# Chunk-selected attention with an ELU MLP on one core: V through the hardware DMA queue with a cast on GpSimd, and weight loads split and queued behind the casts

## The chip, the cores and the metric

The kernel runs on one core of one Trainium2 chip. The time is the device time of one execution in microseconds (us). A "span" is the time from the first to the last instruction of the one profiled execution. All profiled executions shown here are fast runs.

## The reference, cut to what matters

Attention over 4 batches of 8 heads, sequence 768, head dimension 64. For each query, an upper bound of the score is computed for each chunk of 32 keys (from the chunk's minimum and maximum), and only the six best chunks take part. The result, 3072 tokens of 512, goes through an MLP.

```python
k_min = np.min(k_chunks, axis=3); k_max = np.max(k_chunks, axis=3)
ub = np.sum(np.maximum(q[:, :, :, None, :] * k_min[:, :, None, :, :], q[:, :, :, None, :] * k_max[:, :, None, :, :]), axis=-1)
top_chunks = np.argsort(np.where(causal, ub, -1e9), axis=-1)[..., -6:]
...                                   # masked softmax over the selected chunks
attn @ v                              # (4, 8, 768, 64) -> x (3072, 512)
h = x @ w_in                          # (512, 2048)
g = np.where(h > 0, h, np.exp(np.minimum(h, 0)) - 1)
return g @ w_out                      # (2048, 512)
```

Inputs are fp32; V is 6.3 MB and the two weight matrices are 8.4 MB together.

## The kernel before

Heads are handled in 16 pairs. `load` brings K and Q of a pair, `prep` transposes them on TensorE, `select` makes the selection mask of two pairs, and `attend` computes scores, softmax and output. A scheduler orders each engine's queue at build time, so the order of the code is not the order of the queues.

K and Q come over SyncE's hardware queue (called the SP queue below); V and the weights are cast from fp32 to bf16 while they are transferred, which is done from GpSimd's software queue:

```python
def load(t):
    ...
    for h in range(2):
        nc.sync.dma_start(out=k_pair[:, :, h, :], in_=k[b, 2 * r + h].rearrange("(n p) d -> p n d", p=P))
    for h in range(2):
        nc.sync.dma_start(out=q_pair[:, :, h, :], in_=q[b, 2 * r + h].rearrange("(n p) d -> p n d", p=P))

def load_v(t):
    for h in range(2):
        nc.gpsimd.dma_start(out=vexts[t % NSET][:, :, h, 0:D], in_=v[b, 2 * r + h].rearrange("(n p) d -> p n d", p=P))
```

The mask reaches the score matmul's operands through four small DMAs (27 KB each) that stand on the same SP queue as K and Q:

```python
def select(g):
    ...
    nc.vector.transpose(out=selT, in_=sb[:, :, :].rearrange("p b c -> p (b c)"))
    for j in range(2):
        s = (2 * g + j) % NSET
        nc.sync.dma_start(out=rhsA[s][64:64 + NCH, Q0:S], in_=selT[64 * j:64 * j + NCH, :])
        nc.sync.dma_start(out=rhsB[s][0:NCH, Q0:S], in_=selT[64 * j + 32:64 * j + 32 + NCH, :])
```

The weights are loaded almost at once:

```python
def prep_group(g):
    for j in range(2):
        t = 2 * g + j
        if t + 2 < npairs:
            lds[t + 2] = load(t + 2)
        load_v(t)
        prep(t)

prep_group(0)
load_w_in()
select(0)
prep_group(1)
load_w_out()
for g in range(ng):
    attend(2 * g)
    ...
```

The softmax here doesn't subtract the row's maximum and nothing guards it: scores larger than these inputs give would overflow.

## Time and profile before

| reading | value |
|---|---|
| time, median of 3 | 397.43 us (396.59 to 397.96) |
| span of the profiled run | 394.6 us |
| TensorE (PE) busy | 317.5 us, 80% |
| PE busy before 60 us | 23.7 us |
| PE busy after 60 us | 294 of 335 us, 88% |

The first fence is from the profile page: the span in 40 slices of 9.9 us; a digit is the busy share in tenths, PEclk the granted TensorE clock in tenths, DMA the mean busy share of the 16 DMA engines in tenths, and the last row the GB/s that they moved.

```profile
PE   1562068678869869999998788999999988979886
PEclk9995559959998989999999699999999999999999
DMA  9999993543643733930233034101100010200102
GB/s 174 209 186 189 192 207 21 85 108 24 87 104 21 113 81 26 173 94 2 80 28 26 2 26 54 53 2 45 38 13 2 27 53 2 80 2 35 44 2 80
```

In the first six slices the DMA engines are busy all the time and PE is nearly idle in slices four and five. The next fence is the timeline of that stretch: start, length, engine ("SPq" is the SP queue issuing a DMA), line, operation; at the end the idle time before it and what ended it. Lines 82 and 85 load K and Q, lines 217 and 218 the mask.

```profile
16.18 9.96 SPq L85 DMA_DIRECT2D q_pair<-in_q_dram  x2
26.26 5.23 SPq L82 DMA_DIRECT2D k_pair<-in_k_dram  x2
28.02 0.77 DVE L214 STREAM_TRANSPOSE selT<-selb_171 128x576 bf16<-128x576 bf16 x1
31.59 9.38 SPq L85 DMA_DIRECT2D q_pair<-in_q_dram  x2
41.07 5.13 SPq L82 DMA_DIRECT2D k_pair<-in_k_dram  x2
46.30 0.86 SPq L217 DMA_DIRECT2D rhsA_119<-selT  x1
49.00 0.58 PE L243 MATMUL sps<-rhsA_119,lhsA_117 128*128 128x384 bf16 x2 [15.38 <-DMA rhsA_119<-selT]
```

The mask selT is ready at 28.8 us. Its DMA is issued at 46.3 us, because the loads of q3, k4, q4 and k5 (pair 3's Q, pair 4's K and so on) stand before it in the in-order queue, and each of these lines, two issues of 192 KB, takes 5 to 10 us where an unhindered one takes about 1.1 us. PE waits 15.4 us for the mask.

### The profile page before, as it was taken

The numbers are of one execution on the slowest core, as the hardware profiler recorded it, in microseconds if no ns is written. First come the engines' busy times: TensorE is split into PE (matmuls) and PEld (weight loads), VectorE is DVE, ScalarE is ACT, GpSimd is POOL, SyncE is SP. The second block draws the span as 40 slices with busy tenths as digits, with TensorE's granted clock in tenths as the row PEclk, the third lists the DMA queues.
The fourth block names the chain that finished last, engine by engine and source line by source line (L and its number), as shares of the span: only waits on it lengthen the run. The fifth ranks groups of instructions, "written<-read, shape, count | busy, mean of one in ns | idle before, by whom it ended". The sixth has DMA issues, their size and how long they took to land.

```text
span 394.6 us, 6477 instructions
## 1 busy us (share of the span) xinstructions
PE 317.5 (80%) x2272; PEld 175.1 (44%) x2272; DVE 205.0 (52%) x594; ACT 226.5 (57%) x489; POOL 116.2 (29%) x244
## 2 busy tenths in 40 slices
PE   1562068678869869999998788999999988979886
PEld 1331034444544545554555454554556444444442
DVE  7462026637638737555286396372686345252550
ACT  2633086696896894785378956672589143251430
POOL 7651001201413322243033233251133134151430
PEclk9995559959998989999999699999999999999999
DMA  9999993543643733930233034101100010200102
GB/s 174 209 186 189 192 207 21 85 108 24 87 104 21 113 81 26 173 94 2 80 28 26 2 26 54 53 2 45 38 13 2 27 53 2 80 2 35 44 2 80
DMA packets 82592, 27.52 MB, mean 70 GB/s; under 512 B 76160, under 2 KB 78976, under 8 KB 82560
## 3 DMA queue, kind: packets, MB, share of 16 engines
q1 hardware_dynamic: 54784, 19.77, 20.4%
q0 software_dynamic: 27776, 7.34, 18.2%
q8 instruction: 18, 0.29, 0.3%
q14 instruction: 14, 0.11, 0.1%
HBM read 27.26 MB, written 6.29 MB: 85 GB/s over the span
## 4 chain that ended last, share of the span: by engine, by line
issue 30%; PE 24%; ACT 18%; POOL 16%; DVE 8%; SPq 3%; DMA 1%; POOLq 0%; ACTq 0%
POOL m_sb L301 13%; PE o_ps L308 9%; ACT pt L246 5%; PE sps L243 4%; PE ub L200 3%; DVE gT L303 2%; PE h_ps L295 2%; SPq L85 2%; PE psK L162 2%; PE psQ L182 2%; ACT QTf L187 1%; SPq L82 1%; ACT e_sb L299 1%; ACT rhsB_120 L189 1%; ACT lhsB_118 L169 1%
## 5 line engine op out<-in xcount | busy, mean ns | idle before, releaser
L295 PE MATMUL h_ps<-xt,w_in_sb 128*128 128x384 bf16 x512 | 105.3, 327 | 12.1 <-DVE gT L303 11.5
L301 POOL TENSOR_SCALAR m_sb<-e_sb 128x384 f32<-128x384 f32 x128 | 65.6, 516 | 155.2 <-ACT e_sb L299 143.8
L246 ACT ACTIVATE pt<-sps 128x384 bf16<-128x384 f32 (+1 forms) x160 | 80.4, 534 | 53.4 <-PE sps L243 51.5
L303 DVE SCALAR_TENSOR_TENSOR gT<-h_ps,m_sb 128x384 bf16<-128x384 f32 x128 | 70.4, 554 | 41.4 <-POOL m_sb L301 38.1
L308 PE MATMUL o_ps<-w_out_sb,gT 128*128 128x512 bf16 x384 | 88.1, 379 | 0.0
L299 ACT ACTIVATE e_sb<-h_ps 128x384 f32<-128x384 f32 x128 | 62.3, 496 | 40.4 <-PE h_ps L295 38.6
L295 PEld LDWEIGHTS <-w_in_sb 128*128 128x128 bf16 x512 | 48.3, 97 | 47.3 <-issue 20.2
L308 PEld LDWEIGHTS <-gT 128*128 128x128 bf16 x384 | 37.2, 98 | 40.8 <-issue 1.0
L314 DVE COPY o_sb<-o_ps 128x512 f32<-128x512 f32 x16 | 11.1, 691 | 53.1 <-PE o_ps L308 53.0
L273 PEld LDWEIGHTS <-pt 128*128 128x128 bf16 x672 | 29.3, 103 | 17.5 <-DVE pt L255 8.0
L182 PE MATMUL psQ<-ident_f,q_pair 128*128 128x128 f32 x96 | 21.0, 338 | 17.3 <-ACT lhsB_118 L169 7.3
L162 PE MATMUL psK<-ident_f,k_pair 128*128 128x128 f32 x96 | 19.2, 317 | 11.2 <-DMA k_pair<-in_k_dram 4.6
L312 ACT ACTIVATE o_sb<-o_ps 128x512 f32<-128x512 f32 x8 | 4.8, 597 | 39.0 <-PE o_ps L308 39.0
L190 DVE TENSOR_SCALAR Qrl<-QTf 128x576 f32<-128x576 f32 x16 | 7.5, 469 | 35.1 <-ACT QTf L187 35.1
L182 PEld LDWEIGHTS psQ<-ident_f,q_pair 128*128 128x128 f32 x96 | 12.3, 164 | 28.5 <-ACT lhsB_118 L169 10.1
L243 PE MATMUL sps<-rhsA_119,lhsA_117 128*128 128x384 bf16 (+2 forms) x36 | 9.9, 315 | 18.4 <-DMA rhsA_119<-selT 15.4
L255 DVE TENSOR_TENSOR pt<-pt,tri_168 128x512 bf16<-128x512 bf16 x32 | 13.5, 421 | 13.4 <-ACT pt L246 13.4
L162 PEld LDWEIGHTS psK<-ident_f,k_pair 128*128 128x128 f32 x96 | 11.5, 157 | 19.6 <-ACT rhsB_120 L189 5.6
L249 ACT ACTIVATE pt<-sps 128x512 bf16<-128x512 f32 x32 | 19.3, 604 | 1.4 <-PE sps L243 1.3
L285 DVE COPY xt<-pxt 128x384 bf16<-128x384 bf16 x32 | 11.3, 352 | 16.2 <-PE pxt L284 15.8
L165 DVE TENSOR_REDUCE kmm<-psK 128x12 f32<-128x384 f32 x32 | 17.6, 549 | 3.9 <-PE psK L162 3.4
L166 DVE TENSOR_REDUCE kmm<-psK 128x12 f32<-128x384 f32 x32 | 17.4, 545 | 0.0
(220 smaller groups left out, 418.2 us busy)
## 6 DMA issues: line engine op xcount, KB each, us to landing
k_pair<-in_k_dram SPq DMA_DIRECT2D x32, 192.0 KB
q_pair<-in_q_dram SPq DMA_DIRECT2D x32, 192.0 KB
out_dram<-o_sb SPq DMA_DIRECT2D x24, 256.0 KB
w_in_sb<-in_moe_w_in_dram POOLq DMA_DIRECT2D x4, 512.0 KB, 8.9
w_out_sb<-in_moe_w_out_dram POOLq DMA_DIRECT2D x4, 512.0 KB, 17.3
vext_116<-in_v_dram POOLq DMA_DIRECT2D x8, 96.0 KB, 3.4
vext_122<-in_v_dram POOLq DMA_DIRECT2D x8, 96.0 KB, 3.6
vext_128<-in_v_dram POOLq DMA_DIRECT2D x8, 96.0 KB, 3.4
```

Source lines behind the costliest of these rows:

```text
L162: nc.tensor.transpose(ps[:, P * n:P * (n + 1)], k_pair[:, 3 * h + n], ident_f)
L165: nc.vector.tensor_reduce(out=kmm[:, 0, cs], in_=pv, axis=AX.X, op=AOT.min)
L182: nc.tensor.transpose(ps[:, P * n:P * (n + 1)], q_pair[:, 3 * h + n], ident_f)
L243: nc.tensor.matmul(sps[:, o + pc:o + pc + w], lhsT=lhs[hd][:, P * kb:P * (kb + 1)], rhs=rhs[hd][:, c0:c0 + w], start=True, stop=True)
L246: nc.scalar.activation(out=pt[:, hd, 0:wtot], in_=sps[:, 0:wtot], func=AF.Exp, scale=SCALE)
L249: nc.scalar.activation(out=pt[:, :, 0:256], in_=sps[:, :].rearrange("p (h w) -> p h w", h=2), func=AF.Exp, scale=SCALE)
L273: nc.tensor.matmul(o3[:, hd, qi, :], lhsT=pt[:, hd, P * qt + off:P * qt + off + P], rhs=vexts[s][:, kb, hd, :], start=(kb == 0), stop=(kb ...
L295: nc.tensor.matmul(hw, lhsT=w_in_sb[:, kk, P * fc:P * (fc + 1)], rhs=xT[NPAIR * b + kk][:, ts], start=(kk == 0), stop=(kk == NKK - 1))
L299: nc.scalar.activation(out=e_sb, in_=hw, func=AF.Exp)
L301: nc.gpsimd.tensor_scalar(out=m_sb, in0=e_sb, scalar1=-1.0, scalar2=1.0, op0=AOT.add, op1=AOT.mult)
L303: nc.vector.scalar_tensor_tensor(out=gT[:, fc, :], in0=hw, scalar=0.0, in1=m_sb, op0=AOT.max, op1=AOT.min)
L308: nc.tensor.matmul(o_ps, lhsT=gT[:, fc, P * tt:P * (tt + 1)], rhs=w_out_sb[:, fc, :], start=(fc == 0), stop=(fc == NFC - 1))
```

## The change

The intent is to take V off GpSimd's software DMA and to keep the weights out of the way of the first loads. V is loaded as fp32 over the SP queue and cast on GpSimd; the weights are cut in quarters, queued on GpSimd behind the V casts of pairs 2 to 5; two pools shrink to make room for the fp32 V.

```diff
-    ptpool = pool("ptpool", 14)
+    ptpool = pool("ptpool", 10)
-    xtpool = pool("xtpool", 12)
+    xtpool = pool("xtpool", 10)
+    def load_v(t):
+        b, r = divmod(t, NPAIR)
+        v_pair = ldpool.tile([P, NQT, 2, D], F32, name="v_pair")
+        for h in range(2):
+            nc.sync.dma_start(out=v_pair[:, :, h, :],
+                              in_=v[b, 2 * r + h].rearrange("(n p) d -> p n d", p=P))
+        return v_pair
+    ldv = {t: load_v(t) for t in range(2)}
-    def load_v(t):
-        ...                                   # the casting DMA on GpSimd
+    def cast_v(t):
+        return nc.gpsimd.tensor_scalar(out=vexts[t % NSET][:, :, :, 0:D], in0=ldv.pop(t), scalar1=1.0,
+                                       scalar2=0.0, op0=AOT.mult, op1=AOT.add)
...
+    wload = {2: [lambda: load_w_in(0), lambda: load_w_in(1)],
+             3: [lambda: load_w_in(2), lambda: load_w_in(3)],
+             4: [lambda: load_w_out(0), lambda: load_w_out(1)],
+             5: [lambda: load_w_out(2), lambda: load_w_out(3)]}
     def prep_group(g):
         ...
                 lds[t + 2] = load(t + 2)
-            load_v(t)
+                ldv[t + 2] = load_v(t + 2)
             prep(t)
+            cast = cast_v(t)
+            if t in wload:
+                with tc.issue_after(cast.ins):
+                    for f in wload[t]:
+                        f()
-    load_w_in()
-    load_w_out()
```

More of the change, by code (lines that the diff above doesn't have):

```diff
@@ L106 @@
         kst.append(const.tile([P, 2, 64], F32, name=f"kst{s}"))
-    def load_v(t):
-        b, r = divmod(t, NPAIR)
-        for h in range(2):
-            nc.gpsimd.dma_start(out=vexts[t % NSET][:, :, h, 0:D],
-                                in_=v[b, 2 * r + h].rearrange("(n p) d -> p n d", p=P))
+    def cast_v(t):
+        return nc.gpsimd.tensor_scalar(out=vexts[t % NSET][:, :, :, 0:D], in0=ldv.pop(t), scalar1=1.0,
+                                       scalar2=0.0, op0=AOT.mult, op1=AOT.add)
     for s in range(NSET):
@@ L141, with load_w_in, load_w_out @@
     w_out_sb = const.tile([P, NFC, DMODEL], BF16, name="w_out_sb")
-    def load_w_in():
-        for kk in range(NKK):
-            nc.gpsimd.dma_start(out=w_in_sb[:, kk, :], in_=moe_w_in[P * kk:P * (kk + 1), :])
-    def load_w_out():
-        wo = moe_w_out.rearrange("(k p) f -> p k f", p=P)
-        for i in range(4):
-            nc.gpsimd.dma_start(out=w_out_sb[:, 4 * i:4 * i + 4, :], in_=wo[:, 4 * i:4 * i + 4, :])
+    wi = moe_w_in.rearrange("(k p) f -> p k f", p=P)
+    wo = moe_w_out.rearrange("(k p) f -> p k f", p=P)
+    def load_w_in(i):
+        nc.gpsimd.dma_start(out=w_in_sb[:, :, 512 * i:512 * (i + 1)], in_=wi[:, :, 512 * i:512 * (i + 1)])
+    def load_w_out(i):
+        nc.gpsimd.dma_start(out=w_out_sb[:, 4 * i:4 * i + 4, :], in_=wo[:, 4 * i:4 * i + 4, :])
     qf = {}
```

## The prediction

> **What bounds the kernel now.** Median 397.4 us, profiled span 394.6. The stage table shows two regimes. After 60 us PE is busy 294 of 335 us (88%) and DMA shares fall to 0.1-0.7: PE-bound. Before 60 us PE is busy only 23.7 us while the DMA share is 0.9-1.3 at 176-209 GB/s: DMA-bound.
>
> The timeline shows how this costs time. The first selection mask selT is ready at 28.8 us, but its four small DMAs stand on the in-order SP queue behind q3, k4, q4 and k5. Those issues are back-pressured (q3 10.0 us, k4 5.2, q4 9.4, k5 5.1, against 1.1 us unhindered), because the weights (8.4 MB in HBM) share the DMA engines. The mask is issued at 46.3 us, and the first score matmul starts at 49.0 us after PE idled 15.4 us (releaser: DMA rhsA<-selT).
>
> The Trainium skill, "DMA: Bandwidth & Descriptors", section "Queues, rings and completion order", says each DMA engine round-robins between queue rows; the trace agrees: from 7 to 46 us the SP queue moved only some 3.1 MB (80 GB/s).
>
> **What the change does.**
> - V goes to the SP queue as fp32: 6.3 MB. From the queue table (23.5 ns per hardware packet) and an unchanged 24,600 packets I estimate 2.2 us of all 16 engines per pair, about what V cost before.
> - GpSimd loses two V issues per pair (1.69 us) and gains one 128x768 cast; from the 0.51 us of the 128x384 m_sb I estimate 1.0-1.6 us. Neutral.
> - Weights start only after the cast of pair 2's V, about 20 us instead of 11; w_out's halves wait for attention of pairs 0 and 1.
> - In the built order the first mask DMAs now follow pair 3's V and precede k4. Ahead of them are 4.7 MB. At 190 GB/s with one w_in quarter competing, I estimate they issue at 28-30 us, just as selT is ready, and land by 32-33 us.
> - ptpool 14 to 10, xtpool 12 to 10: somewhat less run-ahead; the built PE order still interleaves much alike.
>
> **On the critical path.** Attention starts at about 33 instead of 49 us: 16 us, and everything behind it shifts. Given back: the second mask sits behind pairs 4, 5, k6 and w_in, which I estimate free at 47-55 us where it is wanted at about 51: 0-4 us; smaller pools and casts in the GpSimd order, 0-3 us. The first w_in columns land near 30 us, before their first matmul; w_out long before use.
>
> **Predicted: 382 us, 80% range 374 to 390. Faster by over 2%: 0.87; within 2%: 0.10; slower: 0.03.**
>
> **What would show each step.** (1) Timeline: first score matmul at 31-35 us, SP issues up to v3 short (1-3 us), selT's DMA issued within 2 us of selT. (2) PE idle before the first score matmul falls from 15 to under 4 us. (3) The cast lasts 1.0-1.6 us and GpSimd is no oftener the releaser. (4) Stage table: DMA share near 1 until 55-60 us; PE busy from attention's start to the end about 294 us over 330-336 us.
>
> **What would make it wrong.** The cast takes far longer (strided bf16 output, DVE beside it) and, in order, delays m_sb or the kst of the next selection; late V delays kst of pair 1, so selT; weights and pairs 4-6 collide and stall group 1's mask or w_in by over 5 us; smaller pools break overlap late, where PE is the limit.

## The result, and the profile after

| | before | after |
|---|---|---|
| time, median of 3 | 397.43 us | 379.73 us (377.84 to 379.96) |
| span of the profiled run | 394.6 us | 378.3 us |
| mask issued / first score matmul | 46.30 / 49.00 us | 28.43 / 34.92 us |
| first score matmul to the end | 345.6 us | 343.4 us |

The ratio is 0.9543 (95% interval 0.9489 to 0.9597). Ratios here are the mean time of one kernel's fast runs over that of the other's fast runs of the same rounds, so they are not quite the ratio of the quoted medians. Executions over 1.5% slower than the fastest of the same kernel are left out of the means. When the changed kernel was run again on another chip it gave 380.46 us and 0.9594 (0.9561 to 0.9627).

The same rows of the page for the changed kernel (slices of 9.5 us):

```profile
PE   1476876889599999599997799999999989979886
PEclk9995697589989999989998999999999999999999
DMA  9949999935914526501000000102000100101002
GB/s 205 277 74 192 203 181 177 280 71 118 209 42 98 125 71 161 117 2 55 30 12 2 1 14 28 58 0 83 5 11 2 57 29 26 58 3 55 28 2 83
```

PE no longer stands still in slices four and five. The DMA engines are busy to about 76 us instead of 60, and rest in slice three. The timeline of the changed kernel (line 93 loads V, 118 is the cast, 154 loads w_in, 189 transposes Q, 224 is the mask, 250 the scores):

```profile
16.23 1.30 SPq L93 DMA_DIRECT2D v_pair<-in_v_dram  x2
18.19 0.84 POOL L118 TENSOR_SCALAR vext_134<-v_pair 128x768 bf16<-128x768 f32 x1
18.97 0.98 POOL L154 DMA_DIRECT2D w_in_sb<-in_moe_w_in_dram  x1
27.64 0.77 DVE L221 STREAM_TRANSPOSE selT<-selb_177 128x576 bf16<-128x576 bf16 x1
28.43 0.86 SPq L224 DMA_DIRECT2D rhsA_125<-selT  x1
34.23 0.90 PE L189 MATMUL psQ<-ident_f,q_pair 128*128 128x128 f32 x3 [0.88 <-ACT lhsB_142 L176]
34.92 0.63 PE L250 MATMUL sps<-rhsA_125,lhsA_123 128*128 128x384 bf16 x2
```

The first weight quarter is issued at 19.0 us, when all loads of pairs 0 to 3 have already been issued (the last one, pair 3's V, took 1.3 us). The mask follows its transpose at once, and PE comes to the first score matmul straight from a transpose, with no wait for the mask.

Of the 16.3 us by which the span shortened, 14.1 us had been gained by the first score matmul (49.00 to 34.92) and 2.2 us after it (345.6 to 343.4). The queue table, before and then after (packets, bytes, time of the packets as a share of 16 engines' span; q1 is hardware, q0 software):

```profile
q1 hardware_dynamic: 54784, 19.77, 20.4%
q0 software_dynamic: 27776, 7.34, 18.2%
```

```profile
q1 hardware_dynamic: 79872, 26.06, 27.7%
q0 software_dynamic: 4224, 4.19, 7.1%
```

Share times span gives 80.5 us (q1) and 71.8 us (q0) before, 104.8 and 26.9 us after: V cost the hardware queue 24.3 us of all engines, 1.5 us per pair, and the software queue lost 44.9 us. The weights are cut differently too (4224 packets remain on q0). The run v_hardware_only below keeps the weights in their old pieces: there q0 has 2688 packets and 6.3% of 389.2 us, 24.5 us, so V had taken 47.3 us of the software queue, 3.0 us per pair.

### The profile page after: what moved, and what is told of

The parts are those of the page before. It is cut to its first block, busy times and chain, and to the rows that moved or that the text cites. A ratio compares the mean times of both kernels' runs of the same rounds, so it can differ in the third digit from the quotient of the medians.

```text
span 378.3 us, 6504 instructions
## 1 busy us (share of the span) xinstructions
PE 318.7 (84%) x2260; PEld 176.6 (47%) x2272; DVE 205.3 (54%) x594; ACT 225.4 (60%) x489; POOL 103.3 (27%) x228
## 3 DMA queue, kind: packets, MB, share of 16 engines
q0 software_dynamic: 4224, 4.19, 7.1%
## 4 chain that ended last, share of the span: by engine, by line
PE 27%; issue 23%; ACT 21%; POOL 12%; DVE 11%; DMA 4%; POOLq 0%; SPq 0%; ACTq 0%; DVEq 0%
POOL m_sb L308 12%; PE o_ps L315 8%; ACT pt L253 6%; PE sps L250 4%; PE ub L207 4%; PE h_ps L302 4%; DMA k_pair<-in_k_dram 2%; DVE gT L310 2%; PE psQ L189 2%; ACT e_sb L306 2%; ACT QTf L194 1%; PE psK L169 1%; DMA rhsA_137<-selT 1%; ACT pt L256 1%; PE pxt L291 1%
## 5 line engine op out<-in xcount | busy, mean ns | idle before, releaser
L302 PE MATMUL h_ps<-xt,w_in_sb 128*128 128x384 bf16 x512 | 108.4, 333 | 13.2 <-DVE gT L310 12.8
L302 PEld LDWEIGHTS <-w_in_sb 128*128 128x128 bf16 x512 | 49.1, 99 | 49.1 <-issue 22.7
L262 DVE TENSOR_TENSOR pt<-pt,tri_174 128x512 bf16<-128x512 bf16 x32 | 14.3, 446 | 12.8 <-ACT pt L253 12.6
```

The lines of the kernel that those rows point to most:

```text
L302: nc.tensor.matmul(hw, lhsT=w_in_sb[:, kk, P * fc:P * (fc + 1)], rhs=xT[NPAIR * b + kk][:, ts], start=(kk == 0), stop=(kk == NKK - 1))
```

## The experiments

**Theory A**: the first mask is late because the weight traffic back-pressures the SP issues that stand ahead of it; what counts is that the weights come later. **Rival B**: V's move frees the DMA engines and GpSimd. **Rival C**: only the mask's place on the SP queue counts, which the new build order happened to move ahead of k4.

### Each half of the change alone

The weights alone: V stays a casting DMA, the pools stay.

```diff
 # kernel before
+            last = nc.gpsimd.tensor_tensor(out=kst[s][rows, 1, cols], ...)   # returned by prep
-            prep(t)
+            last = prep(t)
+            if t in wload:                       # the quarters of the changed kernel
+                with tc.issue_after(last.ins):
+                    for f in wload[t]:
+                        f()
-    load_w_in()
-    load_w_out()
```

> The kernel before with only the weight loads changed: split in quarters and queued on GpSimd behind the kst operations of pairs 2 to 5; V stays a casting DMA on GpSimd, pools 14 and 12. k4, q4 and k5 still precede the first mask on the SP queue. Theory A (the first mask is late because weight traffic back-pressures the SP issues ahead of it): those issues take 1 to 3 us each, the mask is issued within 2 us of selT, near 29 us, first score matmul at 32 to 36 us, 380 us in all (377 to 385). Rival B (moving V off the software queue is what frees the DMA engines and GpSimd): most of the gain is missing, 390 us or more.

Measured: 380.33 us, ratio 0.9596 (0.9567 to 0.9625). Its timeline:

```profile
18.03 3.36 SPq L82 DMA_DIRECT2D k_pair<-in_k_dram  x2
21.49 1.24 SPq L85 DMA_DIRECT2D q_pair<-in_q_dram  x2
22.83 1.28 SPq L82 DMA_DIRECT2D k_pair<-in_k_dram  x2
29.10 0.88 SPq L218 DMA_DIRECT2D rhsA<-selT  x1
33.59 0.63 PE L244 MATMUL sps<-rhsA,lhsA 128*128 128x384 bf16 x2
```

k4, q4 and k5 still stand ahead of the mask, but now they take 1.2 to 3.4 us each and are out of the way by 24.1 us. The first weights leave GpSimd at 30.06 us, after the mask. This is the whole gain of the change, within the intervals, with V untouched. Theory A's numbers held, and B is refuted as the cause of the gain. Rival C is not needed: the place in the queue was not changed.

V alone: the changed kernel with the weights loaded early, in their old pieces.

```diff
 # changed kernel
-            cast = cast_v(t)
-            if t in wload: ...
+            cast_v(t)
     prep_group(0)
+    load_w_in()
     select(0)
     prep_group(1)
+    load_w_out()
```

> The changed kernel with the weights loaded early and in their old pieces; V by hardware fp32 with the GpSimd cast, pools 10 and 10. In its built order the mask follows pair 3's V and precedes k4. Theory A: 4.7 MB stand ahead of the mask and share the engines with 8.4 MB of weights, so the mask is issued at 40 to 46 us, and the time is 393 to 400 us. Rival B: V's path is the gain, 378 to 384 us. Rival C (only the mask's place on the SP queue matters): mask near 29 us, 380 to 386 us.

Measured: 390.42 us, ratio 0.985 (0.9818 to 0.9882), a little under theory A's range and above B's and C's.

```profile
24.50 10.81 SPq L82 DMA_DIRECT2D k_pair<-in_k_dram  x2
35.35 7.24 SPq L85 DMA_DIRECT2D q_pair<-in_q_dram  x2
42.64 1.30 SPq L93 DMA_DIRECT2D v_pair<-in_v_dram  x2
43.96 1.51 PE L169 MATMUL psK<-ident_f,k_pair 128*128 128x128 f32 x6 [10.10 <-DMA k_pair<-in_k_dram]
44.05 0.87 SPq L224 DMA_DIRECT2D rhsA<-selT  x1
48.79 0.63 PE L250 MATMUL sps<-rhsA,lhsA 128*128 128x384 bf16 x2
```

With the weights early, k3 and q3 are held up for 18 us, although the mask now precedes k4. The first score matmul is as late as before, but PE's long wait is another one: 10.1 us for pair 3's K, whose transposes stand ahead of the first scores in this build. No wait for the mask is left when they are done. So what the weights hold up is every load on the SP queue; in the kernel before it is the mask that PE meets first. What this half gains (5.9 us of median) comes after that matmul: 340.4 us from it to the end (389.2 minus 48.79) against 345.6.

### Half of the weights

```diff
 # weights_late_only, but w_in as in the kernel before
+    load_w_in()            # after prep_group(0), old pieces
     wload = {4: [w_out 0, 1], 5: [w_out 2, 3]}
```

> Dose test: the kernel before with w_in early as it was and only w_out (half of the weight bytes) put off behind the kst operations of pairs 4 and 5. Theory A (weight traffic ahead of the mask): about half of the back-pressure goes, the mask is issued at 33 to 39 us instead of 46, and 6 to 13 us of the gain come: 384 to 391 us. If only a total absence of weight traffic helped, 394 us or more.

Measured: 385.04 us, ratio 0.9716 (0.9675 to 0.9757).

```profile
12.10 11.74 SPq L85 DMA_DIRECT2D q_pair<-in_q_dram  x2
34.58 0.88 SPq L219 DMA_DIRECT2D rhsA<-selT  x1
37.38 0.59 PE L245 MATMUL sps<-rhsA,lhsA 128*128 128x384 bf16 x2 [3.78 <-DMA rhsA<-selT]
```

Half of the weight bytes out of the way brings the mask from 46.3 to 34.6 us and about two thirds of the gain. The effect follows the amount of weight traffic, as theory A says. (w_in has its old pieces here, and w_out's pieces are the same in all kernels, so the new cut of the weights does not explain it.)

### The mask's place in the queue

```diff
 # kernel before
-    select(0)
+    mask0 = select(0)      # select returns its last mask DMA
...
+                if g == 1:                        # loads of pairs 4 and 5
+                    with tc.issue_after(mask0.ins):
+                        lds[t + 2] = load(t + 2)
```

> The kernel before with only the loads of pairs 4 and 5 queued behind the first mask on the SP queue. Pair 3's q was issued by 26.1 us in the kernel before, so theory A and rival C say: mask issued at 29 us, landed by 32 to 35 us, first score matmul at 33 to 37 us; k4 to q5 then come by 55 us, before their use: 379 to 386 us. If the weight traffic itself (rather than the place in the queue) is what costs, the gain is under 8 us: 389 us or more.

Measured: 385.36 us, ratio 0.9702 (0.9661 to 0.9744). One of its four runs, 390.2 us, was slow; the ratio uses the three fast ones, 383.0 to 386.4 us.

```profile
13.81 12.77 SPq L85 DMA_DIRECT2D q_pair<-in_q_dram  x2
28.17 0.87 SPq L217 DMA_DIRECT2D rhsA<-selT  x1
32.64 8.99 SPq L85 DMA_DIRECT2D q_pair<-in_q_dram  x2
37.34 0.59 PE L244 MATMUL sps<-rhsA,lhsA 128*128 128x384 bf16 x2 [5.64 <-DMA rhsA<-selT]
```

So the order alone is worth 11 to 12 us. The mask is issued at 28.2 us, but its matmul starts 9.2 us later, 0.3 us outside the expected range, where in the kernel before it was 2.7 us. PE waits for the mask to the end of these 9.2 us: issued early, the small transfer lands slowly while the weights, and the SP queue's own q3 ahead of it, are still under way; how much each of the two holds it up was not separated (from ScalarE's queue, below, it still took 6.2 us). The queue position costs issue time, the traffic landing time. Late weights cure both, as weights_late_only, where PE has no wait for the mask, shows; the new order alone cures only the first.

### The mask on another queue

```diff
-            nc.sync.dma_start(out=rhsA[s]..., in_=selT...)      # and rhsB
+            nc.scalar.dma_start(out=rhsA[s]..., in_=selT...)
```

> The kernel before with only the four mask DMAs of each selection issued from ScalarE's queue instead of SyncE's; weights early, V unchanged. Theory A and rival C both say that the mask then escapes the blocked SP queue: issued near 29 us, landed by 32 to 35 us in spite of the weight traffic, first score matmul at 33 to 37 us, 380 to 388 us. Rival B: no gain, 395 to 400 us. Loss possible: the DMA issues take ScalarE's time, 4 x 0.7 us per selection.

Measured: 409.31 us, ratio 1.0339 (1.0307 to 1.037), slower than the kernel before. The time was a miss, though the first score matmul came at 35.78 us, within the expected 33 to 37. The timeline (ACTq is ScalarE issuing a DMA; the SP issue at 36.41 is the first of two):

```profile
28.58 7.73 SPq L85 DMA_DIRECT2D q_pair<-in_q_dram  x2
29.59 1.32 ACTq L217 DMA_DIRECT2D rhsA<-selT  x1
35.78 0.58 PE L243 MATMUL sps<-rhsA,lhsA 128*128 128x384 bf16 x2 [6.92 <-DMA rhsA<-selT]
36.41 4.83 SPq L82 DMA_DIRECT2D k_pair<-in_k_dram  x1
36.71 0.73 ACTq L218 DMA_DIRECT2D rhsB<-selT  x1
41.61 0.73 ACTq L217 DMA_DIRECT2D rhsA<-selT  x1
47.39 0.74 ACTq L218 DMA_DIRECT2D rhsB<-selT  x1
48.17 0.48 ACT L168 ACTIVATE lhsA<-psK 64x384 bf16<-64x384 f32 x1 [18.58 <-DMA q_pair<-in_q_dram]
```

The first mask DMA left ScalarE at once. The second started 0.4 us after the SP issue of q4 had ended (28.58 + 7.73 = 36.31), the third 0.4 us after the first half of k5 (36.41 + 4.83 = 41.24). It looks as if the two hardware queues took turns behind one shared back-pressured place; that is read off these times and was not tested further. ScalarE's own work stood still for 18.6 us behind its DMA issues, and that ate the early start: the second mask is issued at 69.57 us, against 69.21 in the kernel before. The loss itself comes after that point: 337.7 us from there to the end against 325.4. In each later selection the four issues keep ScalarE from its work again, 2.6 to 2.8 us in the three that were looked at (its idle time before the first activation after the issues, at 72.71, 103.19 and 134.77 us). That fits the loss and the expectation's "4 x 0.7 us per selection", but was not tested alone. Moving a small urgent DMA to a compute engine's queue turned its wait into that engine's wait.

### What the V path is worth

Three runs asked what V's half contributes. The pools alone:

```diff
 # kernel before
-    ptpool = pool("ptpool", 14)
+    ptpool = pool("ptpool", 10)
-    xtpool = pool("xtpool", 12)
+    xtpool = pool("xtpool", 10)
```

> The kernel before with ptpool 14 to 10 and xtpool 12 to 10 and nothing else; the built order on TensorE is unchanged. My prediction charged 0 to 3 us for this together with the casts. Expected: 0 to 2 us slower than before (ratio 1.000 to 1.005). If the smaller pools cost more, the V path is worth more than the run with V alone showed; if it is 0, all of that run's gain belongs to the V path and the instruction order that it brings.

Measured: 396.31 us, ratio 1.0008 (0.998 to 1.0036): nothing.

The cast twice, so that GpSimd spends as long on V as it did on issuing V's DMAs; the built order stays the same:

```diff
 # changed kernel
             cast = cast_v(t)
+            cast = cast_v(t, again=True)      # the same cast once more
```

> The changed kernel with the GpSimd cast of every V pair done twice (0.84 us more GpSimd time per pair, 13.4 us in all; the built order on all engines stays that of the changed kernel). If GpSimd's occupancy by V (1.69 us of issues before, 0.84 us of cast after) is what the V path is worth, this gives the gain back: 383 us or more. If GpSimd has slack and the V path is worth what it is by the instruction order that was built with it, 379 to 381 us.

Measured: 379.56 us, ratio 0.9594 (0.9564 to 0.9625), the same as the changed kernel. GpSimd has slack there, and the time V takes on it does not matter.

V never reloaded (a wrong result, relative error 1.23):

```diff
 # kernel before
+            if t < NSET:
-            load_v(t)
+                load_v(t)
```

> Wrong result on purpose: the kernel before with V loaded only for the first four pairs and never again, so the later V transfers and their GpSimd issues are gone; the weights stay early. The first mask is as late as before (46 us), so theory A expects no more than what the V path can be worth: 388 to 393 us. Its built order interleaves MLP and attention as the changed kernel does. Were V's traffic the main cost, 382 us or less.

Measured: 394.57 us, ratio 0.9972 (0.9938 to 1.0006), outside the expected range. Taking 12 of the 16 V loads away, traffic and issues both, gains 0.6% at most and perhaps nothing. With the weights early, V's later transfers are worth no more than that.

So the 5.9 us that V's half gave when the weights were early belong neither to the pools, nor to GpSimd's time, nor, as far as no_v_reload tells (its built order differs too), to V's later traffic. What remains is the instruction order that the scheduler built with it (for example, in that kernel pair 3's Q is transposed ahead of the first scores), or V's effect in the first 50 us. The traces speak for the order. From the sixth to the eighth mask issue, long after the first 50 us, the kernel before took 83.4 us (204.61 to 288.04) and weights_late_only and pools_only the same, but v_hardware_only took 79.6 us (203.41 to 283.01), the changed kernel 79.6 (192.51 to 272.06) and no_v_reload 79.8. In that stretch PE waits for no V transfer in the kernel before, and v_hardware_only has less PE work in it (72.9 against 75.8 us), so part of the work was done at another time. No run changed the order alone, so this is not shown.

With the weights late, the contribution is offset: weights_late_only and the changed kernel have the same ratio within their intervals, although the changed kernel keeps the 3.8 us of that stretch. It loses 1.3 us at the first score matmul (34.92 against 33.59) and 2.6 us from the second to the third mask issue (30.3 us against 27.8), where the same number of matmul records (176) kept PE busy for 23.5 against 21.3 us, at a mean granted clock of 0.72 against 0.82.

### Is the changed kernel still held up by its DMAs?

Three variants of the changed kernel ran beside it on one chip.

> The changed kernel unedited, on the same chip as the three variants of it below, to compare them with: 379 to 381 us, ratio to before 0.954 to 0.960.

Measured: 380.46 us, ratio 0.9594 (0.9561 to 0.9627).

The second half of the weights still later:

```diff
-             4: [lambda: load_w_out(0), lambda: load_w_out(1)],
-             5: [lambda: load_w_out(2), lambda: load_w_out(3)]}
+             6: [lambda: load_w_out(0), lambda: load_w_out(1)],
+             7: [lambda: load_w_out(2), lambda: load_w_out(3)]}
```

> The changed kernel with w_out's halves queued behind the casts of pairs 6 and 7 instead of 4 and 5. The DMA share from 50 to 75 us falls below 1 and the second mask lands in about 2.6 us instead of 4.4. If the collision of weights with the loads of pairs 4 to 6 still costs (my 0 to 4 us given back), 376 to 378 us; if the kernel is bound by its engines there, unchanged within 1 us of the changed kernel.

Measured: 380.46 us, ratio 0.9592 (0.9547 to 0.9637). The stage from 50 to 60 us of the changed kernel and then of this one (busy us and instructions of PE, PEld, DVE, ACT, POOL, then clock, DMA share, GB/s; the share comes out above 1 in some stages, which reads as busy throughout):

```profile
50.00:60.00 10.00, 6.97 (x79) 4.18 (x76) 7.93 (x35) 4.32 (x9) 2.51 (x4) 1.00 1.04 173
```

```profile
50.00:60.00 10.00, 6.62 (x65) 3.88 (x64) 6.72 (x22) 6.11 (x14) 1.76 (x5) 1.00 0.34 78
```

The DMA share of this stage fell from 1.04 to 0.34 and the time did not move.

The first mask behind k4 and q4, which fills the time in which the SP queue stands waiting for selT (17.5 to 28.4 us):

```diff
+    lds[4] = load(4)
-    select(0)
+    select(0, behind=lastq[4])        # mask DMAs traced under issue_after(q4's last DMA)
+    ldv[4] = load_v(4)
```

> The changed kernel with the first mask queued behind k4 and q4: the SP queue stood idle from 17.5 to 28.4 us waiting for selT, and now loads 0.79 MB in that time. If the head-of-line wait costs later, 1 to 3 us faster than the changed kernel; if the transfers of pairs 4 and 5 have slack, unchanged within 1 us. The mask should still be issued by 30 us.

Measured: 379.91 us, ratio 0.9576 (0.9544 to 0.9609): no difference that these runs resolve. The mask was issued at 27.55 us. In both runs transfers moved and the time stayed, so a busy DMA row after the first mask is by itself no sign of a DMA-bound stage any more. The stage from 30 to 50 us, where w_in is loaded, was not tested.

### A faster version

From 60 to 71 us, where two pairs are prepared, the changed kernel's ScalarE is the busy engine. One of its three evictions per Q transpose was moved:

```diff
-            nc.scalar.activation(out=rhsB[s][64:P, ts], in_=ps[64:P, :], func=AF.Copy)
+            nc.vector.tensor_copy(out=rhsB[s][64:P, ts], in_=ps[64:P, :])
```

> Attempt at a faster version: the changed kernel with one of the three ScalarE evictions of each q transpose (rhsB) on VectorE. ScalarE is busy 94% from 62 to 70 us (preparation of two pairs) while VectorE is busy 43%. If ScalarE bounds these stretches, 3 to 8 us faster than the changed kernel: 372 to 377 us. If not, 378 to 382 us, the work only moved (its built order also differs).

Measured: 369.49 us, ratio 0.9313 (0.9279 to 0.9347), correct, and the fastest of all; the gain is larger than expected. The stage of the changed kernel, then of this one (same columns):

```profile
60.00:71.00 11.00, 7.92 (x42) 4.71 (x40) 4.62 (x12) 10.40 (x25) 1.61 (x7) 0.59 1.22 230
```

```profile
60.00:71.00 11.00, 8.69 (x43) 5.14 (x42) 5.72 (x14) 9.40 (x23) 1.61 (x7) 0.53 1.20 233
```

ScalarE was busy 10.4 of 11 us (10.1 in the run on the same chip) and now 9.4, with the DMA share unchanged at 1.2. But this is not where the 11 us against the changed kernel on the same chip came from: at the third mask issue the new kernel was only 1.0 us ahead (82.15 against 83.14). The largest step is the next one: the third to the fourth mask issue took 25.4 us (82.15 to 107.53) against 29.9 us (83.14 to 113.01). These stages, in whole us, of the changed kernel on the same chip (after_again) and of this one:

```profile
83.00:113.00 30.00, 24.73 (x219) 15.32 (x218) 19.32 (x64) 24.77 (x57) 8.99 (x21) 0.94 0.51 116
```

```profile
82.00:108.00 26.00, 22.66 (x213) 13.94 (x211) 21.50 (x67) 22.74 (x53) 7.98 (x19) 1.00 0.62 141
```

ScalarE's work in it fell by 2.0 us, PE's by 2.1 us, and the granted clock was 1.00 instead of 0.94. The built order differs too. How much of the gain is ScalarE's relief, how much the order and how much the clock is not separated.

## Why the prediction was right or wrong, point by point

The prediction was 382 us; 379.73 was measured. The total is closer than its terms, which is partly luck: attention started 1.9 us later than forecast, and what follows became 2.2 us shorter where up to 7 us longer was allowed for.

- **"DMA-bound before 60 us", mask blocked by back-pressured SP issues**: the blocking is right, and shown by the dose of weights (mask issued at 46.3, 34.6 and 29.1 us with all, half and none of the weight load in the way).
- **"they issue at 28-30 us, just as selT is ready"**: 28.43 us, 0.02 us after the end of the transpose.
- **"Attention starts at about 33 instead of 49 us: 16 us"**: 34.92, so 14.1 us. PE was not waiting for the mask; its order put pair 3's transposes first.
- **"Weights start only after the cast of pair 2's V, about 20 us"**: 18.97 us.
- **"Given back: ... 0-4 us ... 0-3 us"**: both terms were too large. The second mask was issued at 53.91 us, when its transpose ended (53.88), so the queue was free, and PE waited 0.6 us for it (its matmul at 58.30); w_out_later and k4_q4_before_mask found nothing to gain. Pools and casts cost nothing (1.0008; double_cast equal). The rest of the kernel became 2.2 us shorter instead of longer.
- **"one 128x768 cast ... I estimate 1.0-1.6 us"**: 0.84 us. The step that failed is scaling the 0.51 us of the 128x384 m_sb by the width, and above it, fixed cost included. If both operations have the same fixed cost and rate, which no run tests, the two durations (0.84 and 0.51 us) give an estimate: the extra 384 columns cost 0.32 us, 0.84 ns each, and some 0.19 us is fixed. At the 1.2 GHz that the Trainium skill, "GPSIMD Engine Reference", section "1. Specifications", gives for GpSimd, this is about 1.0 cycle per column. The same page, section "3.1 Elementwise — side-by-side cycle accounting", has a rate of 1.03 cycles per element for short loop bodies that are bound by the ports; the estimate comes near it. GpSimd's share of the chain that ended last fell from 16% to 12%, so it is no oftener the releaser, as forecast.
- **V "about what V cost before"** in DMA time: 1.5 us per pair on the hardware queue, not 2.2, against 3.0 on the software queue. The term was mis-sized. That it had little effect is likely from no_v_reload (0.3%), where V's later transfers were dropped altogether.
- **"DMA share near 1 until 55-60 us"**: it lasted to about 76 us, with a gap at 20 to 30 us (share 0.40) that I had not foreseen: the SP queue stands waiting for selT with the next loads behind it. The check beside it, 330 to 336 us from attention's start to the end, was inconsistent with the prediction's own sum (382 minus 33 is 349); measured 343.4, with PE busy for 302 of them.
- **The credit**: the prediction told the weights' delay and the new order of the mask in one step. The experiments part them: the weights alone give all of it, the order alone two thirds, and the V path, the larger part of the edit, nothing measurable once the weights are late.

The Trainium skill, "DMA: Bandwidth & Descriptors", section "Queues, rings and completion order", says that each DMA engine round-robins between the queue rows that have work. The runs here agree in that the queues slow each other: a mask issued into the traffic had its matmul 9.2 us later instead of 2.7 us, and the mask is issued at 46.3, 34.6 and 29.1 us with all, half and none of the weights early on GpSimd's queue. They do not tell turn-taking from another way of sharing. The section "Issuing engines are not separate DMA queues" says that DMAs from all engines run on the same 16 DMA engines and interleave; mask_on_act_queue agrees with that: issued from ScalarE's queue, the mask still took 6.2 us to its first matmul (29.59 to 35.78 us), PE waiting for it, against 2.7 us from the SP queue in the kernel before.

## What to carry to other kernels

Look for the first small transfer that the compute engines wait for, and see what stands before it on its queue and what shares the DMA engines with it: bulk loads whose use is far off should be issued after it. Before crediting a change of two parts, run each part alone; here the simple part, issuing the weights later, was all of it. Once the wait is gone, a full DMA row may mean nothing; look next at the busiest compute engine of the stage, and measure whether relieving it pays.

## What the Trainium skill lacked or had wrong

- "DMA: Bandwidth & Descriptors", section "Issuing engines are not separate DMA queues", says that issuing from several engines saves the sequencer's time to initiate a DMA, "which is usually small relative to the DMA itself". Under load here it was not small: two 192 KB issues took up to 12.8 us on SyncE's queue. Issued from ScalarE's queue, only the first mask DMA left at once; the next started at 36.7, 41.6 and 47.4 us, and ScalarE's work stopped for 18.6 us.
- The same page gives no figure for how much a hardware queue takes before its issuer blocks. In the changed kernel two 192 KB issues took 1.0 to 1.9 us before the first weights were issued (19.0 us), and 1.0 to 5.4 us from then to 70 us; in the kernels with early weights two took up to 12.8 us. How much the queue holds was not measured.
